# Staged rows of a spectral transform: other places, an earlier leave, wider spacing, and operand tails by a mask

## The chip, the cores and the metric

One core of one Trainium2 chip. The metric is the device time of one execution in microseconds (us); several executions are taken and the median is given. The engines named here: PE (matrix multiply; PEld is its weight load), DVE (vector), ACT (activation and scaled copies), POOL (here it issues the DMAs that add into memory, and clears buffers) and SP (it issues the plain DMAs). Each engine works through its own list in order, and engines wait for each other and for DMAs by semaphores.

## The reference

Two branches are mixed by a gate. All tensors are float32; S = 2048 tokens, D = 576 features, 4608 hidden features.

```python
x = A_x                                                   # 1 x 2048 x 576
g = sigmoid((x * gate_w).sum(-1, keepdims=True))
X = fft.rfft2(x, axes=(-2, -1)) * (A_w_r + 1j * A_w_i)
a = fft.irfft2(X, s=(S, D), axes=(-2, -1))
h = gelu(B_x @ B_w_gate, approximate=True) * (B_x @ B_w_up)
b = h @ B_w_down
return g * a + (1 - g) * b
```

## The kernel before, in words

**The dense branch is PE's work.** Operands are split into a high and a low part (for x: xhi, xlo and a tail xtl; for the weights: the two halves of a `gu` or `dn` buffer), and a product takes high x high, low x high and high x low. Tokens come in two halves of 1024 (p = 0, 1), each in two blocks of 512 (tb = 0, 1). The main loop runs over passes n. A pass takes two blocks of 128 hidden features through gate and up products (four chains of 14 matmuls, lines 780 to 787, into the banks pgu or px), a gelu on ACT, the product on DVE, the split into `hb`, and for the pass before it four down products of 12 matmuls (line 841) into pdn. ACT evicts pdn, scaled by omg = 1 - g, into `stg` (line 866), and a DMA adds it to `yd[u]`, the result of token block u in memory (line 854; u = 0 to 7 are the first half of the tokens, 8 to 15 the second). This is called a put. The passes are counted from 0; passes 33 to 37 are those that matter here, and pass 37 is the last one.

From there on the second half of the tokens goes by product blocks (`products`): seven products of sums and differences of quarter operands instead of eight plain ones. Each of the seven takes two `seven` chains (seven matmuls each, lines 1048 to 1051), with up to two down products behind it. Their operands are a11, a12, a22 and the sums s1 to s4. `operands()` makes them beforehand, in three rounds i = 0, 1, 2 from quarters that SP loads into `wide` (wide<-xs, line 937), in a new tile `sx` that takes over the memory of `til`; `last_operand()` makes s4 at the start of the first product block. Round i = 2 makes tails of which, by partitions, one quarter of 32 holds the high part and the next the low part. `tail_of` does this with a copy on ACT, a subtraction on DVE, and two copies of 32 partitions on ACT. `stacked` does it for halves of 64 partitions with two mask columns of `msk` on DVE.

**The spectral branch is DVE's work in between.** It is a generator (`spectral`): forward row transforms, column transforms (with matmuls, line 293), then `inverse_rows(h)` for both halves of the token blocks. It uses the buffers `rows`, `til` (16 tiles `st[i]`), `tmp` (2672 columns; columns 0 to 1535 are scratch of the row stages), `xraw` (2048 columns) and `wide` (2320 columns). Row stages are lines 92 to 130 (butterflies, twiddles), 465 to 469 (nine-point part) and 501 to 507. `inverse_rows(0)` scales eight rows of 576 columns by the gate (DVE line 622 for rows 0 to 3, ACT line 621 for rows 4 to 7) into `st[0]` to `st[7]`, the staged rows, and POOL adds them to yd[0] to yd[7] (line 626). `inverse_rows(1)` does the same for yd[8] to yd[15], one row at a time in two places of `tmp` (lines 614 and 615); which row comes next is the one whose last put is nearest to eleven gaps ago. Between the two, `inverse_rows(1)` runs its stages woven with `operands()` (`woven`).

**The order is written out by `gap`.** Every chain calls `gap()` twice, every `seven` and every down product once: a pass has 12 gaps, a full product block 22 (14 and 8). A gap first issues what was registered for it (`at(n, fn)`: n gaps from now; `seq(key, (n, fn), ...)`: steps that `due(key)` pulls forward when they are needed), then one of `aux`, and then steps of the generator while `credit` is positive. `credit` grows with the time of the matmuls issued (`tick`, by the factor `rate`: 1.08 in the passes, 0.95 in the product blocks), is capped at 3.0, and each step takes off its cost (the number that it yields); other work on DVE takes off its cost as well. A step that yields None ends the gap. So the order of the instructions on each engine is settled when the program is built; on the chip each engine runs as far ahead as its waits let it.

In pass 33 the staging of the first half takes gaps 1 to 4. The DMAs are registered behind it, so they come in gaps 8 to 15 (`at(3 + t)`, t = 0 to 7). The puts of yd[0] and yd[1] come ahead of gaps 7 and 8 of that pass, those of yd[2] and yd[3] ahead of gaps 11 and 12. SP's order behind this is: the quarters for operands (line 937), four loads into `xraw` (line 1211), and the next weights (lines 730 and 731). The first product block begins behind pass 37 with a `due` of the last h, then totals (line 1028) and splits (lines 1035, 1036) of the weight quarters, `prep_b`; `load_b` loads quarters for the next block, some of them into `tmp` and `wide` where s4's sources lay.

Of the kernel before, what the change touches and what calls it, by code (L numbers as in the profile page):

```python
# [15 lines left out]
P = 128  # L16
S = 2048
D = 576
# [40 lines left out]
def _constants():  # L59
    k = _freqs()  # L60
    m = np.arange(64)
    col = np.zeros((2, 16, P, 2, 2, P))
    for kb in range(16):
        for al in range(2):
            th = 2 * np.pi * (((2 * m[:, None] + al) * (kb + 16 * m[None, :])) % S) / S
            for d, t in ((0, -th), (1, th.T)):
                for l, x in enumerate(_split(_complex_matrix(t))):
                    col[d, kb, :, al, l] = x

    p = np.arange(P)  # L70
    msk = np.zeros((P, 2 + 96))
    msk[:, 0] = np.where(p < 64, 1.0, -1.0)
    msk[:, 1] = np.where(p < 64, 0.0, 1.0)
    th = 2 * np.pi * np.arange(1, 4)[:, None] * np.arange(16)[None, :] / 64
    msk[:, 2:] = np.stack([np.cos(th), np.sin(th)], 1).reshape(1, 96)
    sgn = np.tile(np.where(k > 288, -1.0, 1.0), (P, 1))
    return dict(col=col.reshape(2, 16, P, 512), msk=msk, sgn=sgn)

# [98 lines left out]
def _build(nc, tc, a):  # L177
    with ExitStack() as ctx:
# [5 lines left out]
        def mk(n, shape, dt=F32):  # L184
            return pool.tile([P] + shape, dt, name=n, tag=n)

        def f(x):
            return x.bitcast(F32)
# [16 lines left out]
        gs = mk("gs", [NB])  # L205
        gate = mk("gate", [NB])
        omg = mk("omg", [NB])
        msk = mk("msk", [2 + 96])
        wide_tile = mk("wide", [2 * SW + 4 * NK])
        misc = wide_tile[:, 0:2 * SW]  # L210
        cns = wide_tile[:, 2 * SW:].rearrange("p (q k) -> p q k", q=4)
# [19 lines left out]
        def copy(o, i):  # L231
            act.activation(o, i, AF.Copy)  # L232

        def stacked(o, x):

            vec.tensor_scalar(x, x, msk[:, 1:2], None, op0=ALU.mult)
            vec.scalar_tensor_tensor(o, f(o), msk[:, 0:1], x, op0=ALU.mult, op1=ALU.add)

        st = [til[:, SW * i:SW * (i + 1)] for i in range(16)]

# [360 lines left out]
        def inverse_rows(h):  # L601
            rows = rows_tile()
            T, R = spread(h, rows)
            pl.memset(rows.rearrange("p (c k) -> p c k", c=2)[:, :, 8 * KF:], 0.0)
            yield from moved(lambda t, c: (R[:, c, t, 0:KF], T[:, t, c, 0:KF]))
            yield from woven(inverse_stages(rows), operands() if h else iter(()))
            R = rows.rearrange("p (k t) -> p t k", t=8)
            if h == 1:
                todo_t = list(range(8))
                while todo_t:  # L610
                    t = min(todo_t, key=lambda t: abs(count[0] - added[8 + t] - 11))
                    todo_t.remove(t)
                    o = tmp[:, D * (len(todo_t) % 2):][:, 0:D]
                    vec.tensor_scalar(o, R[:, t, 0:D], gs[:, 8 + t:9 + t], None, op0=ALU.mult)
                    at(2, lambda t=t, o=o: pl.dma_start(yd[8 + t], o, accum_op=ALU.add))
                    yield 0.8
                    for _ in range(3):
                        yield None
                return
            for t in range(4):  # L620
                act.activation(st[t + 4][:, 0:D], R[:, t + 4, 0:D], AF.Copy, scale=gs[:, t + 4:t + 5])
                vec.tensor_scalar(st[t][:, 0:D], R[:, t, 0:D], gs[:, t:t + 1], None, op0=ALU.mult)
                yield 0.85
                yield None
            for t in range(8):
                at(3 + t, lambda t=t: pl.dma_start(yd[t], st[t][:, 0:D], accum_op=ALU.add))
            yield None

        def load_rows(rows, h):
# [37 lines left out]
        def at(n, fn):  # L667

            later.append((count[0] + n, fn))
            later.sort(key=lambda x: x[0])  # L670
# [268 lines left out]
        def operands():  # L939

            sx = pool.tile([P, 16 * SW], F32R, name="sx", tag="til")
            parts = [sx[:, 2048 * i:2048 * (i + 1)].rearrange("p (l t k) -> p l t k", l=2, t=2) for i in range(3)]
            tails = [sx[:, 6144 + TB * i:6144 + TB * (i + 1)] for i in range(6)]
            for i in range(3):
                ops["s1 s2 s3".split()[i]] = (parts[i][:, 0], parts[i][:, 1], tails[i])
            ops["a11"] = (xhi[0][:, 0:2], xlo[0][:, 0:2], tails[3])
            ops["a12"] = (xhi[0][:, 2:4], xlo[0][:, 2:4], tails[4])
            ops["a22"] = (xhi[1][:, 2:4], xlo[1][:, 2:4], tails[5])
            a11, a12, a21, a22 = quarter
            for i in range(3):  # L950
                load_xs(i)
                for _ in range(5):
                    yield None
                if i == 2:
                    yield from tails_of([(ops[n][2], x) for n, x in (("a11", a11), ("a12", a12), ("a22", a22))])
                for o, x, z, op in ((a22, a21, a22, ALU.add), (a21, a11, a21, ALU.subtract),
                                    (a11, a22, a11, ALU.subtract), (fourth[i], a12, a11, ALU.subtract)):
                    vec.tensor_tensor(o, x, z, op)
                    yield 0.72
                sums = (("s1", a22), ("s2", a11), ("s3", a21))  # L960
                yield None
                if i == 2:
                    yield from tails_of([(ops[n][2], x) for n, x in sums])
                else:
                    for n, x in sums:
                        copy(ops[n][0][:, i], x)
                    yield None
                    yield None
                    for n, x in sums:
                        vec.tensor_tensor(ops[n][1][:, i], x, f(ops[n][0][:, i]), ALU.subtract)  # L970
                        yield 0.72

            ops["done"] = True
# [3 lines left out]
        def last_operand():  # L977

            hi, lo = xhi[1][:, 0:2], xlo[1][:, 0:2]
            ops["s4"] = (hi, lo, xtl[0])  # L980
            tail = tail_of(xtl[0], fourth[2])

            def high():
                for i in range(2):
                    copy(hi[:, i], fourth[i])
                next(tail)

            def low():
                for i in range(2):
                    vec.tensor_tensor(lo[:, i], fourth[i], f(hi[:, i]), ALU.subtract)  # L990
                next(tail)
                credit[0] -= 2.0

            seq("s4", (1, high), (3, low), (5, lambda: next(tail)))

        tsum = wide_tile[:, 768:1536]
        wdr = [raws[:, 2304 + D * i:2304 + D * (i + 1)] for i in range(2)]
# [57 lines left out]
        def products(i, spare, pend):  # L1055
# [31 lines left out]
            for n, (name, nd) in enumerate(zip(("a11", "a12", "s2", "s3", "s1", "a22", "s4"), downs)):  # L1087
                m = n + 2
                prep_b(i + m // 7, m % 7)
                if n == 2:  # L1090
                    due("s4")
                if n in (2, 5):
                    for q in (0, 1) if n == 2 else (3, 2):
                        load_b(i + 1, q)
                if n in (2, 3):
                    w = (j + n - 2) % 4
                    copy(dn[w][:, 0], wdr[n - 2])
                    lower(("dn", j + n - 2), dn[w], wdr[n - 2], 0.76)
                if n == 4:
                    due(("dn", j))  # L1100
                    due(("dn", j + 1))
                    load_d(i + 1)
                ps = [ps_one() if n % 2 else ps_gu() for _ in range(2)]
                for s in range(2):
                    seven(ps[s], i, n, name, s)
                    due({1: ("c12", i - 1), 3: ("c21", i - 1), 4: ("c11", i), 6: ("c22", i)}.get(n))
                    if n == 0:
                        copy(u[s], ps[s])
                    for o, x in (((), ((c, u),), ((u, u),), ((u3, u),), ((c, u3), (u, u)), ((u3, u3),), ((c, u),))[n]):
                        add(o[s], x[s], ps[s])  # L1110
                k = {1: ("c11", c), 4: ("c22", c), 5: ("c21", u3), 6: ("c12", c)}.get(n)
                if k:
                    finish(*k)
                for _ in range(nd):
                    if pend:
                        d, t = pend.pop(0)
                        down(d, t)
                        if t == 3 and len(d) > 4:
                            spare.extend(d[4])
                if i == NT // 2 - 1 and n == 5:  # L1120
                    load_last(1)
# [99 lines left out]
        for n in range(4 * NBLK):  # L1221
# [45 lines left out]
                        at(3, lambda q=q: load_w(q))  # L1267
            if state == 2 and tb == 1:
                assert ops["done"], count
                load_b(i + 1, 3)  # L1270
                prep_b(i + 1, 1)
            prev = (p, i, tb, ((j, h0, key0), (j + 1, h1, key1)))
# [71 lines left out]
```

## Time and profile before

| | |
|---|---|
| three runs | 1386.38, 1388.50, 1389.06 us; median 1388.5 |
| the profiled execution | 1389.35 us, its span 1387.6 us, mean granted clock 0.992 |
| busy in the span | PE 1360.7 us, DVE 1181.7, ACT 705.1, POOL 266.0 |
| DMA | 216.02 MB, mean 156 GB/s |

The span reaches from the first to the last instruction; the execution's own time is 1.75 us longer. A timeline row gives start, duration, engine, line of the kernel, operation, output and inputs, the number of instructions merged in the row, and in brackets how long the engine idled before it and what ended that. A row with a count over one is merged, and its duration runs from its first start to its last end. The view of waits lists who waited for whom: us in total, times, the longest. Consecutive matmuls overlap, so that their distance, not their duration, is their price.

### The profile page before, as it was taken

The numbers are of one execution on the slowest core, as the hardware profiler recorded it, in microseconds if no ns is written. First come the engines' busy times: TensorE is split into PE (matmuls) and PEld (weight loads), VectorE is DVE, ScalarE is ACT, GpSimd is POOL, SyncE is SP. The second block draws the span as 40 slices with busy tenths as digits, with TensorE's granted clock in tenths as the row PEclk, the third lists the DMA queues.
The fourth block names the chain that finished last, engine by engine and source line by source line (L and its number), as shares of the span: only waits on it lengthen the run. The fifth ranks groups of instructions, "written<-read, shape, count | busy, mean of one in ns | idle before, by whom it ended". The sixth has DMA issues, their size and how long they took to land.

```text
span 1387.6 us, 20167 instructions
## 1 busy us (share of the span) xinstructions
PE 1360.7 (98%) x7448; PEld 1202.0 (87%) x7448; DVE 1181.7 (85%) x1753; ACT 705.1 (51%) x1108; POOL 266.0 (19%) x330
## 2 busy tenths in 40 slices
PE   9999999999999999999969899999999999999998
PEld 7888888888898888888868788888888788888888
DVE  6999999998888879999868988888888777777776
ACT  5553434446655673443636555555555455555552
POOL 0011111122222211211231011111112221111110
PEclk9999999999999999999989999999999999999999
DMA  9366765688999966665896366666767787676776
GB/s 332 125 136 115 180 98 114 116 186 204 243 265 272 249 158 104 115 116 113 175 209 149 107 154 126 129 126 131 129 125 138 142 147 129 129 131 132 130 176 172
DMA packets 99665, 216.02 MB, mean 156 GB/s; under 512 B 12144, under 2 KB 22384, under 8 KB 99184
## 3 DMA queue, kind: packets, MB, share of 16 engines
q0 software_dynamic: 45568, 93.41, 44.6%
q1 hardware_dynamic: 54000, 121.34, 27.7%
q8 instruction: 58, 0.95, 0.3%
q14 instruction: 39, 0.32, 0.1%
HBM read 113.64 MB, written 93.91 MB: 150 GB/s over the span
## 4 chain that ended last, share of the span: by engine, by line
PE 92%; DVE 3%; DMA 2%; issue 1%; ACT 1%; POOL 0%; SPq 0%; DVEq 0%; POOLq 0%; ACTq 0%
PE pdn L841 31%; PE pgu L780 6%; PE pgu L782 6%; PE pgu L781 6%; PE pgu L1048 4%; PE pgu L1049 4%; PE pgu L1050 4%; PE px L780 3%; PE px L782 3%; PE px L781 3%; PE px L1049 3%; PE px L1048 3%; PE px L1050 3%; PE pgu L1051 2%; PE px L293 2%; PE px L1051 2%
## 5 line engine op out<-in xcount | busy, mean ns | idle before, releaser
L854 POOL DMA_DIRECT2D yd<-stg x264 | 226.9, 863 | 1023.4 <-ACT stg L866 975.5
L866 ACT ACTIVATE stg<-pdn,omg 128x576 f32<-128x576 f32 x272 | 201.8, 742 | 397.3 <-PE pdn L841 263.9
L841 PEld LDWEIGHTS pdn<-dn,hb 128*128 128x128 f32 x2616 | 364.2, 189 | 24.7 <-ACT stg L866 11.2
L841 PE MATMUL pdn<-dn,hb 128*128 128x288 f32 x2616 | 372.6, 296 | 12.8 <-ACT stg L866 11.0
L780 PE MATMUL pgu<-xhi,gu 128*128 128x512 f32 x384 | 150.1, 391 | 0.0
L782 PE MATMUL pgu<-xlo,gu 128*128 128x512 f32 x384 | 149.8, 390 | 0.0
L781 PE MATMUL pgu<-xhi,gu 128*128 128x512 f32 x384 | 149.6, 390 | 0.0
L841 PEld LDWEIGHTS pdn<-dn,gu 128*128 128x128 f32 x816 | 112.0, 188 | 2.6
L841 PE MATMUL pdn<-dn,gu 128*128 128x288 f32 x816 | 113.6, 295 | 0.0
L232 ACT ACTIVATE gu<-raws 128x768 fp32r<-128x768 f32 (+3 forms) x95 | 92.9, 977 | 31.3 <-PE px L786 21.9
L782 PEld LDWEIGHTS pgu<-xlo,gu 128*128 128x128 f32 x384 | 72.1, 188 | 15.7
L780 PE MATMUL px<-xhi,gu 128*128 128x512 f32 x216 | 84.5, 391 | 0.0
L782 PE MATMUL px<-xlo,gu 128*128 128x512 f32 x216 | 84.2, 390 | 0.0
L781 PE MATMUL px<-xhi,gu 128*128 128x512 f32 x216 | 84.1, 389 | 0.0
L780 PEld LDWEIGHTS pgu<-xhi,gu 128*128 128x128 f32 x384 | 72.1, 188 | 12.7
L781 PEld LDWEIGHTS pgu<-xhi,gu 128*128 128x128 f32 x384 | 72.1, 188 | 12.6
L1066 DVE TENSOR_TENSOR xraw<-xraw 128x512 f32<-128x512 f32 x68 | 47.1, 693 | 28.4 <-ACT xraw L1074 27.4
L1083 DVE TENSOR_TENSOR xraw<-gl,px 128x512 f32<-128x512 f32 x68 | 46.6, 687 | 25.8 <-PE px L1051 23.8
L1083 DVE TENSOR_TENSOR gl<-gl,pgu 128x512 f32<-128x512 f32 x68 | 46.5, 683 | 21.6 <-PE pgu L1051 21.6
L818 ACT ACTIVATE gl<-pgu 128x512 f32<-128x512 f32 x48 | 28.6, 597 | 71.1 <-PE pgu L787 69.0
L1049 PE MATMUL px<-xhi,gu 128*128 128x512 f32 x136 | 53.9, 396 | 3.5 <-DVE gu L1035 3.5
L1048 PE MATMUL pgu<-xhi,gu 128*128 128x512 f32 x136 | 54.0, 397 | 3.4 <-ACT gu L232 3.4
(215 smaller groups left out, 2851.5 us busy)
## 6 DMA issues: line engine op xcount, KB each, us to landing
yd<-stg POOLq DMA_DIRECT2D x264, 288.0 KB, 5.1
raws<-wgu SPq DMA_DIRECT2D x36, 640.0 KB, 5.1
raws<-wd SPq DMA_DIRECT2D x72, 288.0 KB, 2.9
raws<-ws SPq DMA_DIRECT2D x38, 384.0 KB, 5.5
colm<-col POOLq DMA_DIRECT2D x32, 256.0 KB, 6.4
wide<-ws SPq DMA_DIRECT2D x20, 384.0 KB, 5.1
tmp<-wf SPq DMA_DIRECT2D x16, 290.0 KB, 6.3
wide<-til SPq DMA_DIRECT2D x64, 72.5 KB, 5.2
```

The lines of the kernel that those rows point to most:

```text
L232: act.activation(o, i, AF.Copy)
L780: pe.matmul(ps, w[:, 0, k, c], xhi[tb][:, k], start=k == 0, stop=False)
L781: pe.matmul(ps, w[:, 1, k, c], xhi[tb][:, k], start=False, stop=False)
L782: pe.matmul(ps, w[:, 0, k, c], xlo[tb][:, k], start=False, stop=False)
L841: pe.matmul(ps[half], h[:, l, c], d[:, q, half * HD:(half + 1) * HD], start=part == 0 and n == 0, stop=part == 1 and n == 2)
L854: pl.dma_start(yd[u], o, accum_op=ALU.add)
L866: put(u, lambda o: act.activation(o.rearrange("p (c k) -> p c k", c=2), v[:, :, 0:HD], AF.Copy, scale=omg[:, u:u + 1]), i == 0)
L1048: pe.matmul(ps, hi[:, c], xh[:, t], start=t == 0, stop=False)
L1049: pe.matmul(ps, lo[:, c], xh[:, t], start=False, stop=False)
L1050: pe.matmul(ps, hi[:, c], xl[:, t], start=False, stop=False)
L1051: pe.matmul(ps, w[:, 512 + P * s:512 + P * (s + 1)], xt, start=False, stop=True)
L1083: vec.tensor_tensor(o, x, v, ALU.add)
```

## The change

- The eight staged rows of the first half lie in `wide` (rows 0 to 3), `xraw` (4 to 6) and `tmp` from column 1536 on (7) instead of in `til`. Their DMAs are registered as the rows are made: row t in two gaps (t = 0 to 3), row t + 4 in six, so that they come in gaps 3 to 6 and 7 to 10 of pass 33.
- The tails of s1, s2, s3 and s4 are made by `stacked` with two more mask columns, for quarters of 32 partitions. Behind the copies of the three sums come two empty steps instead of one. s4's parts come in gaps 2 and 5 instead of 1, 3 and 5, the deadline for them and the loads of the first two weight quarters one product later (n = 3 instead of 2).
- A staged row of the second half has seven empty steps behind it instead of three.
- 3.0 is taken off the credit at the end of the last pass, and s4 takes off 2.6 instead of 2.0.

```diff
-    msk = np.zeros((P, 2 + 96))
+    msk = np.zeros((P, 2 + 96 + 2))
...
-    msk[:, 2:] = np.stack([np.cos(th), np.sin(th)], 1).reshape(1, 96)
+    msk[:, 98] = np.where(p % 64 < 32, 1.0, -1.0)
+    msk[:, 99] = np.where(p % 64 < 32, 0.0, 1.0)
+    msk[:, 2:98] = np.stack([np.cos(th), np.sin(th)], 1).reshape(1, 96)
...
-        def stacked(o, x):
-            vec.tensor_scalar(x, x, msk[:, 1:2], None, op0=ALU.mult)
-            vec.scalar_tensor_tensor(o, f(o), msk[:, 0:1], x, op0=ALU.mult, op1=ALU.add)
+        def stacked(o, x, c=0):
+            vec.tensor_scalar(x, x, msk[:, c + 1:c + 2], None, op0=ALU.mult)
+            vec.scalar_tensor_tensor(o, f(o), msk[:, c:c + 1], x, op0=ALU.mult, op1=ALU.add)
...
                     yield 0.8
-                    for _ in range(3):
+                    for _ in range(7):
                         yield None
                 return
+            x = xraw.rearrange("p q k -> p (q k)")
+            places = [wide_tile[:, D * t:D * (t + 1)] for t in range(4)]
+            places += [x[:, D * t:D * (t + 1)] for t in range(3)] + [tmp[:, 1536:1536 + D]]
             for t in range(4):
-                act.activation(st[t + 4][:, 0:D], R[:, t + 4, 0:D], AF.Copy, scale=gs[:, t + 4:t + 5])
-                vec.tensor_scalar(st[t][:, 0:D], R[:, t, 0:D], gs[:, t:t + 1], None, op0=ALU.mult)
+                act.activation(places[t + 4], R[:, t + 4, 0:D], AF.Copy, scale=gs[:, t + 4:t + 5])
+                vec.tensor_scalar(places[t], R[:, t, 0:D], gs[:, t:t + 1], None, op0=ALU.mult)
+                at(2, lambda t=t: pl.dma_start(yd[t], places[t], accum_op=ALU.add))
+                at(6, lambda t=t: pl.dma_start(yd[t + 4], places[t + 4], accum_op=ALU.add))
                 yield 0.85
                 yield None
-            for t in range(8):
-                at(3 + t, lambda t=t: pl.dma_start(yd[t], st[t][:, 0:D], accum_op=ALU.add))
             yield None
...
                 if i == 2:
-                    yield from tails_of([(ops[n][2], x) for n, x in sums])
+                    for n, x in sums:
+                        copy(ops[n][2], x)
+                    yield None
+                    yield None
+                    for n, x in sums:
+                        stacked(ops[n][2], x, 98)
+                        yield 1.2
...
-            tail = tail_of(xtl[0], fourth[2])
             def high():
                 for i in range(2):
                     copy(hi[:, i], fourth[i])
-                next(tail)
+                copy(xtl[0], fourth[2])
             def low():
                 for i in range(2):
                     vec.tensor_tensor(lo[:, i], fourth[i], f(hi[:, i]), ALU.subtract)
-                next(tail)
-                credit[0] -= 2.0
-            seq("s4", (1, high), (3, low), (5, lambda: next(tail)))
+                stacked(xtl[0], fourth[2], 98)
+                credit[0] -= 2.6
+            seq("s4", (2, high), (5, low))
...
-                if n == 2:
+                if n == 3:
                     due("s4")
-                if n in (2, 5):
-                    for q in (0, 1) if n == 2 else (3, 2):
+                if n in (3, 5):
+                    for q in (0, 1) if n == 3 else (3, 2):
                         load_b(i + 1, q)
...
             if state == 2 and tb == 1:
                 assert ops["done"], count
+                credit[0] -= 3.0
                 load_b(i + 1, 3)
```

More of the change, by code (lines that the diff above doesn't have):

```diff
@@ L207, in _build @@
         omg = mk("omg", [NB])
-        msk = mk("msk", [2 + 96])
+        msk = mk("msk", [2 + 96 + 2])
         wide_tile = mk("wide", [2 * SW + 4 * NK])
```

## The prediction

> **What bounds the kernel now.** I read the page's first part, then PE's waits, then the timeline around each wait.
>
> ```profile
> span 1387.6 us, 20167 instructions
> PE 1360.7 (98%) x7448; PEld 1202.0 (87%) x7448; DVE 1181.7 (85%) x1753; ACT 705.1 (51%) x1108; POOL 266.0 (19%) x330
> ...
> PE pdn L841 <- ACT stg L866: 11.0, 1, 11.0
> PE px L1049 <- DVE gu L1035: 3.5, 1, 3.5
> PE pgu L1048 <- ACT gu L232: 3.4, 2, 3.1
> ```
>
> PE is busy 1360.7 of 1387.6 us. The change takes no matmul away, so it can only win or lose in the other 26.9 us, and in the matmuls that run slowed behind an idle stretch. The waits (line waited for: us in total, times, longest) name three places; each belongs to one part of the change.
>
> **Place 1, the first half's staged rows.** Timeline rows (start us, us, engine, line, operation); the last row is of the DMA list, with us to landing at its end.
>
> ```profile
> 668.60 0.69 PE L841 MATMUL pdn<-dn,hb 128*128 128x288 f32 x4
> 687.71 3.35 PE L841 MATMUL pdn<-dn,hb 128*128 128x288 f32 x24
> 706.81 3.25 PE L841 MATMUL pdn<-dn,hb 128*128 128x288 f32 x12 [10.98 <-ACT stg L866]
> 719.61 0.82 PE L841 MATMUL pdn<-dn,hb 128*128 128x288 f32 x5
> ...
> 704.46 1.67 ACT L232 ACTIVATE sx<-wide 128x512 fp32r<-128x512 f32 x3 [13.71 <-DMA yd<-til]
> 716.41 1.27 ACT L232 ACTIVATE gu<-raws 128x1280 fp32r<-128x1280 f32 x1 [1.25 <-PE px L786]
> 662.40 1.47 DVE L622 TENSOR_SCALAR til<-rows,gs 128x576 f32<-128x576 f32 x2
> 685.95 1.41 DVE L958 TENSOR_TENSOR wide<-wide 128x512 f32<-128x512 f32 x2
> ...
> 676.37 0.86 POOL L626 DMA_DIRECT2D yd<-til  x1 [0.67 <-DMA yd<-stg]
> 686.16 0.85 POOL L854 DMA_DIRECT2D yd<-stg  x1 [5.35 <-issue]
> 693.65 3.83 POOL L626 DMA_DIRECT2D yd<-til  x4
> ...
> 662.93 1.98 SPq L937 DMA_DIRECT2D wide<-xs  x4
> 664.95 2.13 SPq L1211 DMA_DIRECT2D xraw<-xt  x4
> 669.48 0.33 SPq L730 DMA_DIRECT2D raws<-wgu  x1
> ...
> raws<-wgu SPq DMA_DIRECT2D x36, 640.0 KB, 5.1
> ```
>
> ACT's copies into sx, which takes over the tile buffer, wait 13.71 us for the last staged add out of it; the evictions of pdn stand behind them in ACT's order, and PE waits 10.98. A pass normally lasts 687.71 - 668.60 = 19.1 us; this one lasts 719.61 - 687.71 = 31.9. Its price is 12.8 us, slowed matmuls included.
>
> The adds were late for two reasons. They are queued in gaps 8 to 15, counted from the first gap of pass 33 (staging fills gaps 1 to 4). And there they are interleaved with the puts of the same rows: put 2 stands right behind staged row 2 and idles 5.35 us (686.16), put 3 likewise, so the last four leave only at 693.65.
>
> After the change no staged row lies in the tile buffer. sx then waits only for the row moves that read it, done before the adds of today begin. ACT does the three copies 13.71 us earlier; the stall of 12.8 us goes. The new POOL order, from the code: rows 0 to 3 in gaps 3 to 6, then put 0, row 4, put 1, rows 5, 6, 7, puts 2 and 3. No put follows the same row's add by less than four entries, so no chain of landings is left. The count of instructions and DMAs is the same: eight scalings, eight adds.
>
> The places have new tenants, on SP: wide<-xs (issued at 662.93 today) must now wait for rows 0 to 3, xraw<-xt (664.95) for rows 4 to 6, and raws<-wgu (669.48) stands behind both. Rows 5 to 7 leave behind put 1, as row 0 does today at 676.37. Four adds in a burst took at most 704.46 - 693.65 = 10.8 us to land, so SP is free by about 676.4 + 10.8 = 687, 18 us later than now. The weights of raws<-wgu are read at 716.41, which becomes 716.41 - 12.8 = 703.6; 687 plus 2.1 for issuing xraw<-xt plus 5.1 to land leaves some 9 us. Row 3 is scaled by 662.40 + 1.47 = 664, so wide<-xs starts by 675 or 676 and lands by 681; it is first read at 685.95. Cost nothing; if the cover were gone, ACT's cast of the weights is late and PE with it. Value 12.8; ends 12.8 and 12.8 - 6 (rival 2).
>
> **Place 2, the first product block.**
>
> ```profile
> 773.85 0.53 PE L841 MATMUL pdn<-dn,hb 128*128 128x288 f32 x2 [1.75 <-DVE hb L826]
> 774.21 0.40 PE L1048 MATMUL px<-xhi,gu 128*128 128x512 f32 x1
> 778.12 0.80 PE L1049 MATMUL px<-xhi,gu 128*128 128x512 f32 x1 [3.51 <-DVE gu L1035]
> ...
> 782.04 0.40 PE L1048 MATMUL px<-xhi,gu 128*128 128x512 f32 x1
> 782.27 0.40 PE L1049 MATMUL px<-xhi,gu 128*128 128x512 f32 x1
> ...
> 739.55 0.49 DVE L236 TENSOR_SCALAR xraw<-xraw,msk 128x512 f32<-128x512 f32 x1 [0.75 <-ACT xtl L232]
> 740.07 0.75 DVE L237 SCALAR_TENSOR_TENSOR xtl<-xtl,msk,xraw 128x512 fp32r<-128x512 f32 x1
> 762.13 1.89 DVE L919 TENSOR_TENSOR sx<-wide,sx 128x512 fp32r<-128x512 f32 x3
> 768.65 4.54 DVE L93 TENSOR_TENSOR rows<-rows 128x1280 f32<-128x1280 f32 x3
> 775.57 1.29 DVE L990 TENSOR_TENSOR xlo<-tmp,xhi 128x512 fp32r<-128x512 f32 x2
> 776.78 0.69 DVE L919 TENSOR_TENSOR xtl<-wide,xtl 128x512 fp32r<-128x512 f32 x1
> 777.38 0.69 DVE L1035 TENSOR_TENSOR gu<-raws,gu 128x512 fp32r<-128x512 f32 x1
> 764.69 3.82 ACT L232 ACTIVATE sx<-wide 32x512 fp32r<-32x512 f32 x6
> ```
>
> DVE is the late engine. PE first waits 1.75 us for the low half of h (L826), then 3.51 for the low half of the second weight slot (L1035). From 778.12 to 782.04 nine matmuls take 3.92 us where 0.23 each (782.04 to 782.27) gives 2.07: slowed, 1.85. Together 7.1 us.
>
> - The mask tails. The three sums lose three subtractions and six quarter copies on ACT (3.82 us, ACT not being the late engine: worth nothing) and get three pairs of mask operations. A pair, from its rows, takes 0.52 + 0.69 = 1.2 us against 1.89/3 = 0.63: DVE +1.7 us ahead of L826. But the planner charges 3 x 1.2 in place of 3 x 0.72, 1.44 more, and its credit then stops one row step (4.54/3 = 1.5) earlier; counting the credits over the last six gaps of pass 37, three L93 are issued there instead of four. Net +0.2: the first wait becomes 1.95.
> - s4. Its low halves move from the third to the fifth gap, behind L1035. What now stands ahead, from 775.57 to 777.38, is 1.8 us: the second wait becomes 3.5 - 1.8 = 1.7. They come back later with 0.5 more for the mask, ahead of the third weight slot, where DVE today idles for PE between its products; s4 is the block's last operand.
> - The 3.0 taken off the credit at the end of pass 37 falls behind L826 and touches neither wait, as no row step is issued in that block today; it only delays the row work. Moving two weight loads one step later leaves two steps before their use: nothing.
> - The clock. PE ran slowed after the wait of 3.51, but not at 774.21 after 1.75. Both remaining waits are nearest to 1.75, so I take 0 and keep 1.85 as the other end. The Trainium skill, "TensorE: Matmul & The Clock Gate", section "What's actually happening", has the clock halve after one idle window of about 3.4 us, which is free-running; by it two waits of 1.95 and 1.7 with work between would not fill a window, and the sum would be this one, while if the window also counts their sum as idle it is 1.85 more (rival 4 carries this).
>
> Left: 1.95 + 1.7 = 3.65 of 7.1; gain 3.4. Ends: 7.1 (all goes) and -1.7 (mask work ahead of L826 with no row step given up, nothing won at s4).
>
> **Place 3, the second half's staged rows.** PE rows at the starts of three blocks, then DVE, then the summary of L615 and of the row work by block.
>
> ```profile
> 1017.96 3.35 PE L841 MATMUL pdn<-dn,gu 128*128 128x288 f32 x24
> ...
> 1053.01 3.35 PE L841 MATMUL pdn<-dn,gu 128*128 128x288 f32 x24
> ...
> 1093.02 3.35 PE L841 MATMUL pdn<-dn,gu 128*128 128x288 f32 x24
> ...
> 1084.27 0.78 DVE L614 TENSOR_SCALAR tmp<-rows,gs 128x576 f32<-128x576 f32 x1 [3.27 <-DMA yd<-tmp]
> ...
> DMA to landing us min/median/max: 4.1/6.1/10.3
> ...
> sum 245.00, DVE 27.92 ACT 0.00 POOL 0.00; mean DVE 3.99 ACT 0.00 POOL 0.00
> ```
>
> A block lasts 1053.01 - 1017.96 = 35.05 us; the one with the staging lasts 1093.02 - 1053.01 = 40.0, 5.0 more. DVE waits 3.27 us to write the fifth row, because the half of the scratch it wants, of two, is still being read: the rows before it come three or four gaps of 35.05/22 = 1.6 us apart, two spacings are 10 to 11 us, and the slowest add took 10.3. With seven empty steps rows come at least seven gaps apart, two of them 22 us: no wait. The end of the row work is also later: 3.0 + 0.6 (s4's new charge) + 1.5 (the step given up) = 5.1 us, at 3.99 us of row work per block of 35 us about 28 gaps, and then 8 x 8 gaps. The fifth row, at 1084.27 today, would come near 1084 - 21 + 45 + 19 = 1127 (28 gaps of delay are 45 us; four spacings of eight gaps instead of the 20 gaps that these four take are 19 more), the last some 40 us behind it, 200 us before the end: nothing waits for it. Value 5.0; ends 5.0 and 0.
>
> **The mask tile** grows from 98 to 100 columns; its load lies on the chain at the start.
>
> ```profile
> 3.56 6.89 DMA msk<-msk
> ```
>
> Two per cent of 6.89 is 0.14 us at most; at least 0. I take 0.
>
> **Sum.** 12.8 + 3.4 + 5.0 = 21.2 us. The profiled execution took 1389.35 us, which gives 1368.1; it stands 0.85 above the median of the runs, 1388.5. I predict 1368.
>
> **Rivals.**
> 1. Slower: the adds hold SP. If every add and put waited for the landing of the one before (5.35 us as at 686.16), twelve of them from 661 would last to 725; raws<-wgu would land near 732 instead of by 703.6, 28 us too late, and the kernel would end 28 - 21.2 = 7 us slower, at 1396. It decides once SP is held beyond 703.6 + 21 - 7 = 718. For it: SP is in order and the new tenants are its loads. Against: four adds left within 3.83 us at 693.65 without waiting. Chance 0.03.
> 2. SP held in part: rows 5 to 7 leave as late as 693.65 and land at 704.5; raws<-wgu lands at 710, 6 us late: 1374. For it: puts in POOL's order still wait for their evictions. Against: those evictions no longer wait. 0.08.
> 3. Place 3 keeps its wait, through an add caught behind a put of the same row: 1373. For it: the row chosen is only the nearest to eleven gaps from its put. Against: eight steps of eight gaps in a block of 22 fall on eight different places, each within some four gaps of a choice. 0.09.
> 4. Place 2 gives nothing or gets worse: 1368 + 3.4 to 1368 + 5.1, that is 1371.5 to 1373. For it: DVE has no idle time ahead of L826, and the two waits may slow the clock together. 0.14.
> 5. The change doesn't do what it says: sx still waits for the buffer, through another reader. Only 8.4 us are won: 1381. Against: ACT's wait names yd<-til alone. 0.04.
>
> **How the numbers follow.** The forecast, all three places within 2 or 3 us of the sum, has 0.62; its own range is 1365 to 1371 (place 2 all gone, and slowed). Cases 2, 3 and 4 take the range up to 1375; from 1365 to 1375 leaves out cases 1 and 5 and some of the combinations. 0.2% is 2.8 us, about what a measurement of this kernel can tell from no change. Faster 0.95, within it 0.02, slower 0.03.
>
> **What would show it.** Right: no PE wait for ACT stg near 695 us and passes of 19.1 us throughout; ACT's sx copies without a wait for yd; SP's wide<-xs and xraw<-xt later, raws<-wgu before 690; two PE waits of about 2 and 1.7 us near 760 with full-speed matmuls behind; blocks of 35.05 us throughout, L614 at least 11 us apart. Wrong: PE or ACT waiting for raws or xraw near 700; a wait for L826 of over 3 us; any block of 37 us or more.

## Result and profile after

| | before | after |
|---|---|---|
| median, range | 1388.05 us (1386.38 to 1389.06), 4 runs | 1372.69 us (1370.86 to 1373.47), 4 runs |
| ratio | 1 | 0.9889, 95% interval 0.9872 to 0.9906 |
| profiled execution, its span | 1389.35, 1387.6 us | 1373.01, 1371.2 us |

The change wins 15.4 us. The forecast was 1368, its own range 1365 to 1371, the whole range 1365 to 1375: the time lies where rival 4 had put it (place 2 gives nothing, 1371.5 to 1373). Lines of the kernel after are 3 to 11 higher: L841 is L847, L826 is L832, L1035 is L1046, L614 is L617; L822 (the product of the gelu and the up half) is L828.

The page's first lines after, and PE's list of waits (line waited for: us in total, times, longest):

```profile
span 1371.2 us, 20167 instructions
...
PE 1358.5 (99%) x7448; PEld 1199.6 (87%) x7448; DVE 1184.1 (86%) x1757; ACT 701.0 (51%) x1100; POOL 265.6 (19%) x330
```

```profile
PE px L1060 <- DVE gu L1046: 2.0, 1, 2.0
...
PE pgu L1059 <- DVE gl L828: 1.2, 1, 1.2
PE pdn L847 <- DVE hb L832: 1.2, 1, 1.2
...
PE pdn L847 <- ACT stg L872: 0.6, 1, 0.6
PE pdn L847 <- DVE gu L1081: 0.5, 2, 0.3
```

The wait of 11.0 for ACT is gone, and so is the one of 3.1 for ACT's gu. At the first product block there are now three waits instead of two, one of them on a line (L828) that the prediction did not name.

**Place 1.** Timeline rows of the kernel after (start us, us, engine, line, operation):

```profile
689.89 1.66 ACT L234 ACTIVATE sx<-wide 128x512 fp32r<-128x512 f32 x3
...
702.86 1.28 ACT L234 ACTIVATE gu<-raws 128x1280 fp32r<-128x1280 f32 x1 [1.25 <-PE px L792]
...
707.54 0.63 ACT L234 ACTIVATE xtl<-xraw 128x512 fp32r<-128x512 f32 x1 [3.41 <-DMA xraw<-xt]
...
660.15 2.36 POOL L629 DMA_DIRECT2D yd<-wide  x2
...
674.63 2.07 POOL L630 DMA_DIRECT2D yd<-xraw  x2
675.71 1.87 POOL L630 DMA_DIRECT2D yd<-tmp  x1
...
667.38 6.53 SPq L943 DMA_DIRECT2D wide<-xs  x4
678.29 7.96 SPq L1222 DMA_DIRECT2D xraw<-xt  x4
686.35 0.38 SPq L736 DMA_DIRECT2D raws<-wgu  x1
...
751.39 3.44 PE L847 MATMUL pdn<-dn,hb 128*128 128x288 f32 x24 [0.58 <-ACT stg L872]
```

ACT makes its sx copies without a wait. All eight adds have left by 677.6, and SP is held as forecast: raws<-wgu leaves at 686.35 instead of 669.48 and is still in time, as ACT's cast of it at 702.86 waits for PE alone.

**Place 2.** PE rows, then DVE rows, of the kernel after:

```profile
757.60 0.50 PE L1059 MATMUL pgu<-xhi,gu 128*128 128x512 f32 x1 [1.16 <-DVE gl L828]
...
761.98 0.53 PE L847 MATMUL pdn<-dn,hb 128*128 128x288 f32 x2 [1.15 <-DVE hb L832]
...
764.72 0.80 PE L1060 MATMUL px<-xhi,gu 128*128 128x512 f32 x1 [1.98 <-DVE gu L1046]
765.32 0.63 PE L1061 MATMUL px<-xlo,gu 128*128 128x512 f32 x1
...
770.01 0.63 PE L1062 MATMUL px<-sx,gu 128*128 128x512 f32 x1
...
794.41 3.35 PE L847 MATMUL pdn<-dn,gu 128*128 128x288 f32 x24
...
750.97 1.49 DVE L95 TENSOR_TENSOR tmp<-rows 128x1280 f32<-128x1280 f32 x1
752.50 1.49 DVE L95 TENSOR_TENSOR rows<-rows 128x1280 f32<-128x1280 f32 x1
...
756.87 0.68 DVE L828 TENSOR_TENSOR gl<-gl,pgu 128x512 f32<-128x512 f32 x1
```

The waits sum to 4.3 us (before 5.3). But thirteen matmuls run slowed from 764.72 to 770.44, where it was nine.

**Place 3.** PE rows at the second down group of five blocks, and the summary of the staged rows' adds between 1085 and 1180 us (count, duration in ns, first and last start):

```profile
1046.96 3.35 PE L847 MATMUL pdn<-dn,gu 128*128 128x288 f32 x24
...
1082.05 3.35 PE L847 MATMUL pdn<-dn,gu 128*128 128x288 f32 x24
...
1111.67 2.92 PE L847 MATMUL pdn<-dn,gu 128*128 128x288 f32 x20 [0.26 <-DVE gu L1081]
...
1117.63 3.35 PE L847 MATMUL pdn<-dn,gu 128*128 128x288 f32 x24
...
1153.20 3.35 PE L847 MATMUL pdn<-dn,gu 128*128 128x288 f32 x24
...
1188.25 3.35 PE L847 MATMUL pdn<-dn,gu 128*128 128x288 f32 x24
...
1110.22 0.80 DVE L617 TENSOR_SCALAR tmp<-rows,gs 128x576 f32<-128x576 f32 x1
```

```profile
L618 POOL DMA_DIRECT2D yd<-tmp x8: 1171/1191/1217, 1087.1 to 1172.5; - x8
```

The block of 40.0 us is gone: the five distances between second down groups are now 35.1, 35.1, 35.6, 35.6 and 35.1 (the first from the group before the ones shown, at 1011.87).

**Where the time went**, by the same PE rows in both traces:

| stretch | before | after | won |
|---|---|---|---|
| up to the first down group of pass 33 | 649.50 | 648.74 | 0.76 |
| from there to the second down group of pass 37 (764.20, 751.39) | 114.70 | 102.65 | 12.05 |
| from there to the first group of the second product block (806.84, 794.41) | 42.64 | 43.02 | -0.38 |
| from there to the blocks at 1017.96, 1005.49 | 211.12 | 211.08 | 0.04 |
| five blocks (1024.34 to 1204.56; 1011.87 to 1188.25) | 180.22 | 176.38 | 3.84 |

Together 16.3 of the span's 16.4. The first 0.76 is taken as scatter of the start: the same group stands at 649.62 in a variant below that has the same work ahead of it.

### The profile page after: what moved, and what is told of

The parts are those of the page before. It is cut to its first block, busy times and chain, and to the rows that moved or that the text cites. A ratio compares the mean times of both kernels' runs of the same rounds, so it can differ in the third digit from the quotient of the medians.

```text
span 1371.2 us, 20167 instructions
## 1 busy us (share of the span) xinstructions
PE 1358.5 (99%) x7448; PEld 1199.6 (87%) x7448; DVE 1184.1 (86%) x1757; ACT 701.0 (51%) x1100; POOL 265.6 (19%) x330
## 4 chain that ended last, share of the span: by engine, by line
PE 90%; DVE 6%; issue 1%; DMA 1%; ACT 1%; SPq 0%; DVEq 0%; ACTq 0%
PE pdn L847 30%; PE pgu L786 6%; PE pgu L788 6%; PE pgu L787 6%; PE pgu L1059 4%; PE pgu L1061 4%; PE pgu L1060 4%; PE px L1060 3%; PE px L1061 3%; PE px L1059 3%; PE px L786 3%; PE px L788 3%; PE px L787 3%; PE pgu L1062 2%; PE px L296 2%; PE px L1062 2%
## 5 line engine op out<-in xcount | busy, mean ns | idle before, releaser
L847 PEld LDWEIGHTS pdn<-dn,hb 128*128 128x128 f32 x2616 | 362.8, 188 | 13.8 <-DVE hb L832 1.4
L847 PE MATMUL pdn<-dn,hb 128*128 128x288 f32 x2616 | 371.1, 295 | 1.8 <-DVE hb L832 1.2
L786 PE MATMUL pgu<-xhi,gu 128*128 128x512 f32 x384 | 150.1, 391 | 0.0
L787 PE MATMUL pgu<-xhi,gu 128*128 128x512 f32 x384 | 149.6, 390 | 0.0
L847 PEld LDWEIGHTS pdn<-dn,gu 128*128 128x128 f32 x816 | 112.0, 188 | 3.6 <-DVE gu L1081 1.0
L847 PE MATMUL pdn<-dn,gu 128*128 128x288 f32 x816 | 114.1, 295 | 0.5 <-DVE gu L1081 0.5
L832 DVE TENSOR_TENSOR hb<-gl,hb 128x512 fp32r<-128x512 f32 x76 | 52.1, 685 | 5.9 <-ACT hb L234 5.9
```

The costliest lines, as they stand in the source:

```text
L786: pe.matmul(ps, w[:, 0, k, c], xhi[tb][:, k], start=k == 0, stop=False)
L787: pe.matmul(ps, w[:, 1, k, c], xhi[tb][:, k], start=False, stop=False)
L847: pe.matmul(ps[half], h[:, l, c], d[:, q, half * HD:(half + 1) * HD], start=part == 0 and n == 0, stop=part == 1 and n == 2)
```

## Experiments

All are variants of the kernel after unless said otherwise; lines with a minus are the changed kernel's. Times are medians, with the range of the runs and the ratio to the kernel before on the same chip. The first four variants share one chip, the next four another and the last three a third; the median of the kernel before is 1388.63, 1390.21 and 1388.68 us on them, and 1388.05 in the result above. A difference of 2 us between medians from two chips therefore says little, and the traces decide there. The theories: at place 1, that the time at which the adds leave decides, or, as the rival, the buffer in which the rows lie; at place 3, that the spacing alone removes the stall, or that it goes with the other parts; at place 2, that the mask's added DVE work ate the gain, or the order that the second empty step made, or that row steps fill whatever room there is. A letter in a quoted expectation stands for the theory told beside it there. First place 1 and place 3.

**The first half's staged rows as before the change** (tile buffer, adds registered behind all of them).

```diff
...
-            places = [wide_tile[:, D * t:D * (t + 1)] for t in range(4)]
...
+            places = [st[t][:, 0:D] for t in range(8)]
...
-                at(2, lambda t=t: pl.dma_start(yd[t], places[t], accum_op=ALU.add))
-                at(6, lambda t=t: pl.dma_start(yd[t + 4], places[t + 4], accum_op=ALU.add))
...
+            for t in range(8):
+                at(3 + t, lambda t=t: pl.dma_start(yd[t], places[t], accum_op=ALU.add))
```

> The changed kernel with the staged rows of the first half back in the tile buffer and their adds registered behind the staging, as before; all else as changed. Both theories of place 1: the wait of ACT's sx copies for the adds returns, PE waits about 11 us near 695 us, and the time is 1372.7 + 12.8 = 1385.5 us. If the gain came from elsewhere (other parts of the change), it stays at 1373.

1384.74 us (1383.22 to 1386.29), ratio 0.997 (0.9957 to 0.9983). PE's wait is back:

```profile
PE pdn L845 <- ACT stg L870: 12.2, 1, 12.2
```

**In the tile buffer, but leaving early.** Only the first part of that diff, the places.

> The changed kernel with the staged rows in the tile buffer, but their adds leaving early as in the change (gaps 3 to 10). Theory A (the order on POOL's queue is what counts; in the changed kernel the last add leaves at about 677 us and the sx copies come at 689.9, so the adds are over by then): 1372.7, no wait of ACT for yd beyond 1 us. Theory B (the place is what counts: as long as the rows lie in the tile buffer, sx waits for them): a wait of ACT of 3 to 13 us, 1376 to 1385 us.

1372.19 us (1371.72 to 1373.11), ratio 0.9879 (0.9864 to 0.9894): within 0.5 of the kernel after, 12.55 under the variant above on the same chip. The sx copies again wait for nothing:

```profile
690.78 1.67 ACT L234 ACTIVATE sx<-wide 128x512 fp32r<-128x512 f32 x3
```

So place 1 is worth 12.55 us, and the early leave alone gives all of it. With it, the new places are worth nothing measurable.

**New places, leaving late.** Only the rest of that diff.

> The changed kernel with the staged rows in the new places, but their adds registered behind the staging as before (gaps 8 to 15, between the puts). Theory A (order counts): the last four adds leave near 693 and land near 704; SP's loads into xraw and of the weights stand behind them, the weights land near 711 instead of before 703, and PE waits 5 to 8 us: 1378 to 1381. Theory B (place counts): sx no longer waits, 1372.7.

1399.26 us (1398.89 to 1400.38), ratio 1.0075 (1.0058 to 1.0092). SP's loads into the places now stand ahead of some of the adds, so that rows 3, 5 and 6 are added with the loaded quarters in their places, behind a wait for the load; this makes it no clean test of place against order, and neither figure of the expectation was met. It does show what a queue held by a tenant can cost (POOL, SP, DVE and PE rows):

```profile
690.12 0.86 POOL L632 DMA_DIRECT2D yd<-wide  x1 [1.82 <-DMA wide<-xs]
...
708.15 0.85 POOL L632 DMA_DIRECT2D yd<-xraw  x1 [11.20 <-DMA xraw<-xt]
...
704.42 0.38 SPq L736 DMA_DIRECT2D raws<-wgu  x1
...
717.72 0.69 DVE L964 TENSOR_TENSOR tmp<-wide 128x512 f32<-128x512 f32 x1 [22.10 <-issue]
...
725.75 0.85 PE L847 MATMUL pdn<-dn,hb 128*128 128x288 f32 x2 [15.91 <-DVE hb L832]
```

POOL stands 11.20 us for a load, and row 7 is added out of `tmp` only behind that, at 710.42. DVE stands 22.10 us ahead of its write into `tmp`; the view names no releaser, but by the code the write goes into the columns that row 7 lies in. The split of h (L832) stands behind that write, and PE waits 15.91 for it. The weights leave SP at 704.42, when the prediction needed them landed by 703.6, but PE's long waits are for h and not for them. So this is not rival 1, where SP is held: here POOL is, by SP's load.

**Three empty steps behind a staged row of the second half instead of seven.**

```diff
-                    for _ in range(7):
+                    for _ in range(3):
```

> The changed kernel with three empty steps behind a staged row of the second half instead of seven. Theory C (spacing): the scratch half is wanted again after six or seven gaps, about 10 us, at some row; DVE waits there and PE loses up to 5.0 us: 1375 to 1377.7. Theory D (the wait of before was an accident of which gaps the rows fell on, and the row work's later end removes it): 1372.7.

1375.82 us (1373.52 to 1376.46), ratio 0.9902 (0.9887 to 0.9916). PE rows, and what the summary of the adds says of who waited for them (us, times):

```profile
1080.31 3.35 PE L847 MATMUL pdn<-dn,gu 128*128 128x288 f32 x24
...
1109.18 0.47 PE L1059 MATMUL pgu<-xhi,gu 128*128 128x512 f32 x1 [3.21 <-ACT gu L234]
...
1120.42 3.35 PE L847 MATMUL pdn<-dn,gu 128*128 128x288 f32 x24
```

```profile
  DVE tmp L617: 5.8, 2
```

A block of 40.1 us is back (1120.42 - 1080.31), by DVE waiting for the half of the scratch that is still being read. By the medians the spacing is worth 3.1 us, or 3.6 against the variant in the tile buffer on the same chip; by the traces it is 5.0 less the 1.0 that the kernel after still pays.

**Place 2, part by part.** The tails of s1 to s3 by copies and a subtraction, as before:

```diff
-                    for n, x in sums:
-                        copy(ops[n][2], x)
-                    yield None
-                    yield None
-                    for n, x in sums:
-                        stacked(ops[n][2], x, 98)
-                        yield 1.2
+                    yield from tails_of([(ops[n][2], x) for n, x in sums])
```

> The changed kernel with the tails of s1, s2, s3 made by tail_of again (subtraction on DVE, quarter copies on ACT); s4, credits, staged rows as changed. In the order written out, two row steps L95 then leave gap 447 and stand behind the product L828 again. Theory E (DVE's order ahead of L828, the low half of h and the second weight slot decides): the bank wait of the second seven (1.2 us) goes, the wait for the low half of h is 1.7, for the weight slot 1.7; 1371.5. Theory F (only DVE's total work decides, and it is 0.2 us less here): 1372.5.

1371.17 us (1370.34 to 1371.57), ratio 0.9864 (0.9849 to 0.9878). The wait for L828 is gone; two are left:

```profile
761.19 0.54 PE L847 MATMUL pdn<-dn,hb 128*128 128x288 f32 x2 [1.84 <-DVE hb L832]
...
763.66 0.50 PE L1054 MATMUL px<-xhi,gu 128*128 128x512 f32 x1 [1.70 <-DVE gu L1040]
```

These are nearly the two waits of the prediction (1.95 and 1.7). Place 2 takes 41.15 us here (751.05 to 792.20), 1.87 less than with the mask: 0.75 of that is in the waits' sum (3.54 against 4.29), and 1.15 in the clock, as shown below. Only the 0.75 is surely the mask's, since the clock's share changes between variants with the same waits.

s4 as before (tail by copies and a subtraction, 2.0 off the credit, gaps 1, 3 and 5, weight loads at n = 2):

```diff
...
-            seq("s4", (2, high), (5, low))
+            seq("s4", (1, high), (3, low), (5, lambda: next(tail)))
...
-                if n == 3:
+                if n == 2:
```

> The changed kernel with s4 as before (parts in gaps 1, 3 and 5, subtraction and quarter copies, deadline and loads at n = 2); sum tails by mask. Theory E: the wait for the second weight slot grows from 2.0 by the 1.8 us of s4's low halves to 3.8, and the slowed stretch behind it stays: 1374.5. If the deferral of s4 is worth nothing: 1372.7.

1373.85 us (1373.65 to 1374.26), ratio 0.9884 (0.9869 to 0.9899). The wait for the second slot is 3.8 again: s4's later place is worth 1.8 of wait, and 1.2 of time by the traces (place 2 takes 44.19, 751.49 to 795.68).

The kernel before with the staged rows' parts alone (places, early adds, seven empty steps; the minus is the kernel before here):

```diff
-                    for _ in range(3):
+                    for _ in range(7):
...
+            places = [wide_tile[:, D * t:D * (t + 1)] for t in range(4)]
...
+                at(2, lambda t=t: pl.dma_start(yd[t], places[t], accum_op=ALU.add))
+                at(6, lambda t=t: pl.dma_start(yd[t + 4], places[t + 4], accum_op=ALU.add))
```

> The kernel before with the new places, the early adds and the spacing of eight gaps alone: no mask tails, s4 and credits as before. Theory E, with the trace's finding that the first product block of the changed kernel loses as much as before (7.3 against 7.6 us): 1372.7, within 1 us of the changed kernel, and PE's waits of before at that block (1.75 and 3.5 us). If the mask tails and s4 won the 3.4 us of the prediction there: 1376.

1373.83 us (1372.95 to 1375.23), ratio 0.9887 (0.987 to 0.9903). So mask, s4 and credit together are worth nothing that can be told, where the prediction had 3.4: 1.1 by medians from two chips, nothing by the ratios (0.9887 and 0.9889), and place 2 takes 42.84 here (751.51 to 794.35) against 43.02. On this one chip the variant with copied sum tails, which has s4 and the credit as changed and no mask for the sums, is 2.7 faster than this one.

**No row steps in the last pass while the operands are made**, and 6.0 off the credit behind them:

```diff
                     w = next(other, "end")
                     if w is None:
                         free = count[0]
+                        if quiet[0]:
+                            yield None
...
             ops["done"] = True
+            if quiet[0]:
+                yield 6.0
...
+            quiet[0] = state == 2 and tb == 1
             h0, key0 = hidden(j, tb, lambda: None)
```

> The changed kernel, but while the operands are made in the last pass no row step is issued, and 6.0 is taken off the credit when they are done, so that none stands ahead of the first product block. Theory E and F (DVE's backlog is the whole of it): the waits for L828, the low half of h and the second weight slot go, the slowed matmuls with them: 7.3 us won, 1365.5. Theory G (behind DVE another wait ends just as late: the load of the weight quarter, ACT's copies, or the clock slows anyway): 1368 to 1371, with a new name in PE's waits.

1369.01 us (1368.75 to 1369.83), ratio 0.985 (0.9835 to 0.9864). Place 2 is nearly empty: 751.39 to 788.24, 36.85 us where the kernel after has 43.02. But of these 6.2 us the span keeps 4.2 (1367.0 against 1371.2; 3.7 by medians from two chips), and one new wait stands at 857 us (in the list of waits, and the DVE row ahead of it):

```profile
PE pgu L1065 <- ACT gu L234: 2.7, 3, 2.0
```

```profile
853.87 0.33 DVE L130 SCALAR_TENSOR_TENSOR rows<-rows,tmp 128x160 f32<-128x160 f32 x1 [2.12 <-ACT tmp L116]
```

**The same with 3.0 off the credit instead of 6.0.**

```diff
             if quiet[0]:
-                yield 6.0
+                yield 3.0
```

> As e8 (no row steps in the last pass while the operands are made), but the row work comes back with 3.0 us of credit taken off instead of 6.0. In e8 one wait of 1.97 us stood at 857 us, PE for ACT's cast of gu, with VectorE 2.12 us held there by a twiddle whose scaled copy on ACT came late. If that wait is the accident of where that row step fell, it goes here and the first block is as in e8: 1367 us. If the 6.0 are needed to keep the first products clear of row steps: 1370.5 us, with waits for gl or hb back at 757 to 765 us.

1367.61 us (1366.86 to 1368.28), ratio 0.9849 (0.9835 to 0.9862): the lowest median, 1.5% under the kernel before, its interval clear of the changed kernel's. The wait at 857 is gone, so it belonged to where a twiddle fell, with its scaled copy late on ACT. What is left at place 2 is one wait, behind DVE's wait for a weight quarter that SP issues behind four puts:

```profile
760.92 0.50 PE L1066 MATMUL px<-xhi,gu 128*128 128x512 f32 x1 [1.25 <-DVE gu L1052]
...
759.30 0.96 DVE L1045 TENSOR_TENSOR wide<-wide,raws 128x768 f32<-128x768 f32 x1 [0.33 <-DMA wide<-ws]
```

**The first of these two (6.0) with the sums' tails by copies**, by the line that the diff of the sums' tails adds.

> No row steps in the last pass while the operands are made (as in e8), and the tails of s1 to s3 made with copies and a subtraction as before the change. If the mask's 1.7 us of VectorE still stand ahead of the first product there, as they did with the row steps, this is 1.5 us under e8: 1367.5 us. If without the row steps VectorE has time left and the mask is hidden: the same as e8, 1369 us, within 0.6.

1368.15 us (1367.78 to 1368.25), ratio 0.9853 (0.9839 to 0.9866). Place 2 takes 37.90 (751.02 to 788.92) against 36.85 with the mask, 0.88 of it in a wait for ACT's eviction; so neither of the expected outcomes is clean. Once the row steps are out of the way, the way of making the tails hardly counts.

**One empty step behind the copies instead of two.**

```diff
-                    yield None
                     yield None
                     for n, x in sums:
                         stacked(ops[n][2], x, 98)
```

> The changed kernel with one empty step behind the three copies instead of two; everything else as changed. In its program the three pairs of mask operations (3.6 us of VectorE) come in gap 447 in place of two row steps L95 (2 x 1.49 us) and four twiddles, and row steps follow in gap 450, still ahead of the first product L828. Theory H: it is the second empty step that moved the two L95 ahead of the splits and of L828, so without it the wait for gl L828 (1.2) and most of the slowed matmuls go: 1370.5 us. Theory R: the planner fills whatever credit there is; VectorE has as much work ahead of L828 either way (about 6.9 us in the changed kernel, 7.5 here, from gap 445 on), only in another order: 1372.5 us, within 0.8, with waits of 4 us in sum at the first product block.

1370.12 us (1369.99 to 1371.68), ratio 0.987 (0.9856 to 0.9883).

```profile
758.54 0.50 PE L1058 MATMUL pgu<-xhi,gu 128*128 128x512 f32 x1 [1.90 <-DVE gl L828]
...
762.07 0.54 PE L847 MATMUL pdn<-dn,hb 128*128 128x288 f32 x2 [0.33 <-DVE hb L832]
...
764.53 0.69 PE L1059 MATMUL px<-xhi,gu 128*128 128x512 f32 x1 [1.70 <-DVE gu L1045]
```

The time is that of theory H, the mechanism is not: the wait for L828 grew (1.16 to 1.90), and the three waits sum to 3.9, as theory R has it. The two L95 rows are not to blame as such: here one of them stands ahead of L828 and the three mask pairs stand there too, so that DVE has about as much work ahead of it in another order. The profiled runs differ by 1.3 us in span, and the larger part of it is the clock.

**The clock.** Windows from the end of the last of these waits to the next down group (window: length, PE busy and count, granted clock, DMA share, GB/s), of the kernel before, the kernel after, and four variants: staged rows as before, tile buffer and early leave, three empty steps, and no row steps with 3.0 off the credit.

```profile
778.10:786.10 8.00, 7.98 (x27) 0.76 0.39 137
```

```profile
764.70:773.70 9.00, 8.98 (x27) 0.67 0.09 35
```

```profile
778.70:785.00 6.30, 6.29 (x28) 1.00 0.14 49
```

```profile
764.85:772.40 7.55, 7.55 (x27) 0.81 0.11 41
```

```profile
764.15:772.00 7.85, 7.85 (x27) 0.78 0.11 40
```

```profile
760.90:767.20 6.30, 6.28 (x28) 1.00 0.13 49
```

Each holds the same matmuls, 6.30 us at full clock (a count of 28 takes in the first matmul of the next group). The kernel after pays 2.7 us, its two siblings with the same three waits (about 1.15, 1.15 and 2.0) pay 1.25 and 1.55, and the variant with 0.76, 1.17 and 2.02 pays nothing. The variant with copied sum tails, with two waits of 1.84 and 1.70, pays 1.55 (7.85 us from 763.65 to 771.50, clock 0.78). So the cost is not set by the waits' lengths alone. In two of these the slow matmuls begin only behind the last wait, by 0.8 and 1.3 us, and the slow stretch then lasts 3.4 us (764.45 to 767.83 with copied sum tails, 765.41 to 768.80 with three empty steps). The Trainium skill, "TensorE: Matmul & The Clock Gate", section "What's actually happening", says that the window of about 3.4 us runs freely, so that one kernel can show different numbers of slowed matmuls by its phase. The rows fit this, with 1.25 to 2.7 us behind the same waits and slow stretches of 3.4; that the phase is what decides, no run here shows. With 1.2 us of wait left (the last row) nothing is slowed.

## Why the prediction was right or wrong

- **Place 1, 12.8: right.** The traces give 12.05 and the two variants on one chip 12.55. A new wait of 0.58 for ACT's eviction at 751.39, which the prediction did not have, is already taken off the 12.05. The POOL order, the adds' times and SP's hold came as written (SP free by about 687 in the forecast, raws<-wgu sent at 686.35); rivals 1, 2 and 5 did not occur. The adds' earlier leave is the cause, and not the rows' new places. One of the signs set for being wrong did show: ACT waits 3.41 for xraw<-xt, to 707.54. It is for a fifth load, sent at 701.67, it is 2.59 in the variant with the tile buffer and 1.20 in the kernel before, and PE's groups keep their distances (706.06, 712.44, 725.16), so it cost PE nothing there.
- **Place 2, 3.4: the step that failed.** Measured -0.4 in the stretch of the traces, and nothing that can be told by the variant with the staged rows alone. Two terms failed. The larger is "I take 0" for the clock: 2.7 in the profiled run. The prediction's estimate by that page of the Trainium skill, that two waits with work between would not fill a window, does not hold here: 1.84 and 1.70 slow PE by 1.55, and 1.16, 1.15 and 1.98 by 2.7. The other end that the prediction kept, 1.85, was nearer. The second failed term is "PE first waits 1.75 us for the low half of h (L826)", carried on as 1.95: with the mask a second row step L95 and a mask pair came ahead of the product L828, so that PE waited already for that, 1.16. The wait for the low half of h is 1.15 behind it, and the second slot's is 1.98 instead of 1.7: 4.3 in sum, forecast 3.65. That s4 leaves the second slot's way was right (3.8 with s4 as before, 2.0 without). What place 2 hangs on is DVE's row steps: with them out of the last pass, 6.2 of its 43.0 us go.
- **Place 3, 5.0: right in mechanism, mis-sized.** No wait for the scratch is left, and the rows come 11.1 us apart or more (1110.22 is the third of eight from 1085.78 to 1168.95); the gain is 3.84 by the trace. Rival 3 did not occur. The missing 1.0: in two blocks a staged row's scaling (1110.22, 1145.80) stands right ahead of the split L1081, and PE loses 0.5 each (1111.67). "Blocks of 35.05 us throughout" was 35.6 twice.
- **The sum.** 12.8, 3.4 and 5.0 were 21.2; 12.05, -0.4 and 3.84, with 0.76 of the start, make 16.3 of the span. The forecast took the 21.2 off the profiled execution, 1389.35, which stands 1.3 above the median of the result. The time is 4.7 above the forecast and outside its own range. It lies in the whole range because what rival 4 describes came about, for the two reasons that it gives: DVE late ahead of L826, and waits that slow the clock together. That it falls within rival 4's 1.5 us is in part luck, as place 1 and place 3 fell short by 0.75 and 1.16 as well, and the higher starting point hid 1.3 of it.

## What to carry to other kernels

When a buffer is late to come free, look first at when its readers were queued: moving eight DMAs ahead in the order gave all that moving their buffers seemed to give. A planner that spends credit fills the room ahead of a critical product with other work; to win there, hold that filler back in the stretch. Two or three waits of 1 to 2 us close together cost up to 2.7 us more in clock here, by an amount that changes from variant to variant, so judge them with the granted clock of that window and not by the list of waits.

## What the runs showed that was not expected

- PE ran at about half pace (0.43 us from one matmul to the next, 765.32 to 765.74, instead of 0.23) though no wait in the 20 us before was longer than 1.98.
- Runs of one kernel seem to differ by this too: the kernel after took 1370.86 to 1373.47 us, at a granted clock of 0.999 to 0.998, while the variant without slowed matmuls and with copied tails, at 1.000 in all four runs, took 1367.78 to 1368.25.
